# A long convolution in blocks of 256 steps instead of 128, inside a two-layer H3 and MLP kernel

## The chip, the cores and the metric

The kernel runs on one core of a Trainium2 chip. The metric is the device time of one execution, in microseconds. The core has TensorE (PE; its weight loads are shown apart, as PEld), VectorE (DVE), ScalarE (ACT), GpSimd (POOL), and SyncE (SP), which here issues all the DMAs. Each engine runs its own instructions in the order in which the program issued them.

## The reference

Two layers, each a gated long convolution and then an MLP, on 2048 tokens of 1024 channels, all in float32:

```
x = x + norm(x) * conv(x-independent kv)      # kv = shift_conv4(k) * v, causal conv with ssm_k, plus D * kv
x = x + W2 @ relu(W1 @ norm(x) + b1)**2 + b2  # 1024 -> 3584 -> 1024
```

The convolution `y` of `kv` with the 2048-step kernel `ssm_k`, per channel, takes nothing from x, so it is the same in both layers and is computed once. The reference does it with an FFT over 4096 points.

## The kernel before

The MLP. A unit is one layer on one block of 512 tokens; the eight units run in the order `ORDER = [(0,0),(1,0),(0,1),(0,2),(1,1),(1,2),(0,3),(1,3)]` (layer, block), here called u0 to u7. A unit is some 112 steps; a step uses one tile of 128x512 weights in 12 matmuls. A product of two float32 numbers is made of three fp32r matmuls (`mm3`, L271 to L273) of a high and a low part; ACT makes the high part (L685 for weights, L1030 for the activations), DVE or POOL the low part (L693, L1035). In u0 every weight is split for the first time, and part of them (`split_kept`) is stored as a pair of parts in DRAM (`wd`) and read back later. Raw weights are loaded up to 8 steps ahead into 5 buffers (`wr`).

The convolution. A block of 128 steps is taken into a spectrum with matmuls against 128-point tables of cosines and sines (odd frequencies, `fh`, `fl`); the spectrum of the filter's current block and of the one before it are combined with signs. A complex product is made of three real ones (`PAIRS`). Output block j needs the sum over i of X[i] * G[j - i]: `mult` (L407, POOL, every fourteenth on DVE) writes the products of all i, `red` (L411, DVE) sums them. `fin` then combines the three (L417, L418, POOL), splits the result into a high part yh (L426, ACT) and a low part yl (L430, DVE), transforms it back (six matmuls of 256 columns into a PSUM bank of the ring `pt`), copies it (L447, ACT) and stores it to `yd`. This is done for 16 groups of 64 channels in each of the sequence blocks 1 to 3.

The forward transforms of blocks 1 to 3 are two streams of steps, `fwd_x` (L294 to L328) and `fwd_g` (L349 to L373), in chunks of 128 channels, 24 chunks in all.

The order. Streams are generators; the main loop, at each MLP step, lets them issue as much as `pace` and `FWD_RATE` say, and `Later.at(k, ...)` issues a stage k ticks later, where a tick is one product issued. So the convolution's matmuls stand between the MLP's in TensorE's order, and its DVE and POOL instructions among the others. Blocks 1 and 2 are computed during u0 to u2, block 3 during u3 to u5; `PACE_SLACK` is the number of steps that should be left over. Eighteen steps before the end of a unit that is followed by another block, `close_conv` issues at once whatever is left of the convolution that the next unit needs.

The first block of both convolution and layer 0 (`first_block`) comes ahead of all units. There `Plan` orders the instructions from given costs and chooses DVE or POOL for those that either can do (products L907, sums L909, combinations L913 and L914).

Of the kernel before, what the change touches and what calls it, by code (L numbers as in the profile page):

```python
# [32 lines left out]
Q = 256  # L33
QC = Q // P
QG = Q // CG
PAIRS = ((2, 0), (0, 1), (1, 2))
W_LOAD, W_HI, W_LO, W_PAIR = 8, 4, 3, 5
PAIR_GAP = 10
# [9 lines left out]
PACE_SLACK = 55  # L48
# [8 lines left out]
FWD_RATE = {0: 1.3, 1: 1.2, 2: 1.2, 3: 1, 4: 0.98, 5: 1}  # L57
# [114 lines left out]
def v_cost(n):  # L172
    return 70 + 1.04 * n


def s_cost(n):
    return 130 + 1.04 * n


def g_cost(n):  # L180
    return 160 + 2.1 * n


def a_cost(n):
    return 100 + 0.84 * n
# [3 lines left out]
def tile_h3_mlp(ctx: ExitStack, tc: tile.TileContext, q, kT, vT, shk, ssmT, ssmD, w1, b1, w2, b2,  # L189
# [11 lines left out]

    XD = [dram.tile([NG, P, NBLK, CG], F32, name=f"xd{i}") for i in range(3)]
    GD = [dram.tile([NG, P, NBLK, CG], F32, name=f"gd{i}") for i in range(3)]
    KD = [[dram.tile([P, 2, Q], F32, name=f"kd{sb}_{h}") for h in range(4)] for sb in range(NB - 1)]
# [7 lines left out]
    def mkfx(shape, dt=F32):  # L212
        return cv.tile(shape, dt, name="fx", bufs=6)
# [11 lines left out]
    def const_split(name, src, shape):  # L225
        raw = mkfx(shape)
# [10 lines left out]
    fh, fl = const_split("f", fwd_t, [P, 2, P])  # L237
    ih, il = const_split("i", inv_t, [P, 2, P])
    epst = const.tile([P, 1], F32)
    V.memset(epst, EPS)  # L240

# [33 lines left out]
    def gview(t, h):  # L275
        return t.rearrange("g p b c -> p g b c")[:, QG * h:QG * h + QG]

    def hold(n):
        got = take(n)
        while not got:  # L280
            yield
            got = take(n)
        return got

    def fwd_x(sb, c):
# [17 lines left out]
        ov = o.rearrange("p (g b c) -> p b g c", g=2, b=NT)  # L303
        for b in range(NT):
            PE.transpose(ov[:, b], ks[:, b * P:(b + 1) * P], ident)
# [9 lines left out]
        xo = [mkfx([P, T]) for _ in range(3)]  # L315
        oa = yield from hold(2)
        for r in range(2):
            mm3(oa[r], fh[:, r], fl[:, r], hi, lo, True, True)
        yield
        for r in range(2):  # L320
            A.copy(xo[r], oa[r])
        yield
        V.tensor_add(xo[2], oa[1], xo[0])
        yield
        give(*oa)
        yield
        for i in range(3):
            SY.dma_start(dview(XD[i], sb, c), xo[i].rearrange("p (g b c) -> p g b c", g=2, c=CG))  # L328
        yield

    def dview(t, sb, c):
        return t[2 * c:2 * c + 2, :, NT * sb:NT * sb + NT].rearrange("g p b c -> p g b c")

    def kview(sb, c, r):
        return KD[sb][c // 2][:, r, c % 2 * P:c % 2 * P + P].rearrange("p (g c) -> p g c", c=CG)

    def fwd_g(sb, c):
        raw = mkfg([P, NT, P])
        SY.dma_start(raw, ssmT[sb * T:(sb + 1) * T, c * P:(c + 1) * P].rearrange("(b p) c -> p b c", p=P))
        kk = [mkfk([P, 2, (NT + 1) * CG]) for _ in range(2)]  # L340
        for r in range(2):
            SY.dma_start(kk[r][:, :, 0:CG], kview(sb - 1, c, r))
# [4 lines left out]
        hv, lv = (t.rearrange("p (g b c) -> p b g c", g=2, b=NT) for t in (hi, lo))  # L347
        rv = raw.rearrange("p b (g c) -> p b g c", g=2)
        A.copy(hv, rv)  # L349
        yield  # L350
        V.tensor_sub(lv, rv, hv.bitcast(F32))
# [4 lines left out]
        for r in range(2):  # L356
            mm3(oa[r], fh[:, r], fl[:, r], hi, lo, True, True)
        yield
        og = [o.rearrange("p (g n) -> p g n", g=2) for o in oa]
# [7 lines left out]
        for r in range(2):  # L367
# [968 lines left out]
```

## Time and profile before

| what | value |
|---|---|
| median of 3 runs | 3007.43 us (3004.38 to 3011.22) |
| the profiled execution, its time | 3011.77 us |
| its span, first to last instruction | 3010.0 us |
| mean granted TensorE clock | 0.96 |
| PE, DVE, POOL, ACT busy | 92%, 68%, 44%, 32% of the span |
| HBM read and written | 576.88 MB and 123.73 MB |

A row of the view by stretches gives the stretch, then the busy time of PE, PEld, DVE, ACT and POOL with the number of instructions, then the granted clock as a share of full speed, the busy share of the DMA engines and their GB/s. A row of a group gives line, engine, operation, tiles and shapes, the count, the busy time with the mean in ns, and the idle time of the engine just ahead of these instructions with what ended it. A row of a wait gives who waited for whom, the sum in us, how often, and the longest.

### The profile page before, as it was taken

The numbers are of one execution on the slowest core, as the hardware profiler recorded it, in microseconds if no ns is written. First come the engines' busy times: TensorE is split into PE (matmuls) and PEld (weight loads), VectorE is DVE, ScalarE is ACT, GpSimd is POOL, SyncE is SP. The second block draws the span as 40 slices with busy tenths as digits, with TensorE's granted clock in tenths as the row PEclk, the third lists the DMA queues.
The fourth block names the chain that finished last, engine by engine and source line by source line (L and its number), as shares of the span: only waits on it lengthen the run. The fifth ranks groups of instructions, "written<-read, shape, count | busy, mean of one in ns | idle before, by whom it ended". The sixth has DMA issues, their size and how long they took to land.

```text
span 3010.0 us, 34885 instructions
## 1 busy us (share of the span) xinstructions
PE 2774.8 (92%) x12408; PEld 2268.3 (75%) x12408; DVE 2036.8 (68%) x2624; ACT 972.5 (32%) x1658; POOL 1332.6 (44%) x768
## 2 busy tenths in 40 slices
PE   4668788869999999979999999999999999989999
PEld 3556576758778877858878888888788888878887
DVE  7967789857998799987998779886323322252221
ACT  3433333413334333323322433232223322213221
POOL 4635567635775477765667287737000100030000
PEclk7878899989999999989999999999999999999999
DMA  5457788888788987778876887687445744475444
GB/s 174 156 191 257 232 265 272 269 297 294 251 261 278 337 286 255 258 243 330 273 241 228 278 296 248 219 283 280 159 147 186 277 145 147 143 263 185 139 145 154
DMA packets 339014, 702.96 MB, mean 234 GB/s; under 512 B 75412, under 2 KB 145304, under 8 KB 338840
## 3 DMA queue, kind: packets, MB, share of 16 engines
q1 hardware_dynamic: 338840, 700.73, 69.1%
q8 instruction: 98, 1.61, 0.2%
q14 instruction: 76, 0.62, 0.1%
HBM read 576.88 MB, written 123.73 MB: 233 GB/s over the span
## 4 chain that ended last, share of the span: by engine, by line
PE 53%; DVE 6%; POOL 2%; DMA 2%; issue 1%; ACT 0%; SPq 0%; DVEq 0%; POOLq 0%; ACTq 0%
PE p L271 17%; PE p L273 17%; PE p L272 17%; POOL cp L407 1%; DVE sm L411 1%; DVE whl L693 1%; DMA yt<-yd 1%; DMA whl<-wd_m 1%; DVE fx L297 0%; PE pt L272 0%; PE pt L273 0%; DVE acc L1040 0%; PE pt L271 0%; DVE rl L1035 0%; PE p L582 0%
## 5 line engine op out<-in xcount | busy, mean ns | idle before, releaser
L407 POOL TENSOR_TENSOR cp<-cx,cg 128x320 f32<-128x320 f32 (+11 forms) x535 | 1026.4, 1944 | 637.4 <-DVE sm L411 530.3
L271 PE MATMUL p<-whl,rh 128*128 128x512 f32 x1792 | 718.5, 401 | 23.2 <-DMA whl<-wd_m 12.7
L272 PE MATMUL p<-whl,rh 128*128 128x512 f32 x1792 | 714.4, 399 | 4.3 <-DVE whl L693 4.3
L271 PE MATMUL p<-xh,whl 128*128 128x512 f32 (+1 forms) x1864 | 714.2, 383 | 1.9 <-DMA whl<-wd_m 1.4
L273 PE MATMUL p<-whl,rl 128*128 128x512 f32 x1792 | 713.6, 398 | 0.0
L272 PE MATMUL p<-xl,whl 128*128 128x512 f32 (+1 forms) x1864 | 711.3, 382 | 0.5 <-DVE xl L953 0.3
L273 PE MATMUL p<-xh,whl 128*128 128x512 f32 (+1 forms) x1864 | 710.9, 381 | 0.7 <-POOL whl L693 0.6
L1035 DVE TENSOR_TENSOR rl<-r,rh 128x512 fp32r<-128x512 f32 x224 | 251.6, 1123 | 442.2 <-ACT rh L1030 442.0
L411 DVE TENSOR_REDUCE sm<-cp 128x64 f32<-128x320 f32 (+5 forms) x576 | 473.3, 840 | 54.5 <-POOL cp L407 54.5
L693 DVE TENSOR_TENSOR whl<-wr,whl 128x512 fp32r<-128x512 f32 x397 | 418.9, 1058 | 129.5 <-ACT whl L685 122.8
L685 ACT CAST whl<-wr 128x512 fp32r<-128x512 f32 x400 | 246.7, 619 | 557.3 <-PE p L273 386.0
L271 PEld LDWEIGHTS p<-whl,rh 128*128 128x128 f32 x1792 | 341.9, 191 | 107.3 <-DMA whl<-wd_m 16.8
L271 PEld LDWEIGHTS p<-xh,whl 128*128 128x128 f32 x1864 | 354.9, 190 | 69.3 <-DMA whl<-wd_m 2.1
L273 PEld LDWEIGHTS p<-xh,whl 128*128 128x128 f32 x1864 | 354.2, 190 | 69.2 <-POOL whl L693 1.1
L272 PEld LDWEIGHTS p<-whl,rh 128*128 128x128 f32 x1792 | 342.0, 191 | 84.2 <-DVE whl L693 7.1
L272 PEld LDWEIGHTS p<-xl,whl 128*128 128x128 f32 x1864 | 354.7, 190 | 66.4 <-DVE xl L953 1.0
L273 PEld LDWEIGHTS p<-whl,rl 128*128 128x128 f32 x1792 | 341.5, 191 | 80.0
L1027 ACT ACTIVATE r<-p,b1t 128x512 f32<-128x512 f32 x221 | 152.1, 688 | 685.7 <-PE p L273 683.2
L1040 DVE TENSOR_TENSOR acc<-p,acc 128x512 f32<-128x512 f32 x240 | 160.0, 687 | 188.2 <-PE p L273 187.5
L1149 POOL TENSOR_TENSOR acc<-acc,b2t 128x1024 f32<-128x1024 f32 x24 | 62.5, 2635 | 274.5 <-DMA acc<-x 274.5
L1066 POOL TENSOR_TENSOR px<-xn,px 128x512 f32<-128x512 f32 x8 | 15.2, 1901 | 317.1 <-DVE xn L1065 317.1
L1028 ACT ACTIVATE r<-r 128x512 f32<-128x512 f32 x224 | 141.7, 633 | 7.1
(180 smaller groups left out, 2288.5 us busy)
## 6 DMA issues: line engine op xcount, KB each, us to landing
whl<-wd_m SPq DMA_DIRECT2D x528, 512.0 KB, 4.1
wr<-w SPq DMA_DIRECT2D x408, 256.0 KB, 4.3
wd_m<-whl SPq DMA_DIRECT2D x70, 512.0 KB, 4.9
cx<-xd SPq DMA_DIRECT2D x48, 512.0 KB, 4.5
cg<-gd SPq DMA_DIRECT2D x48, 512.0 KB, 6.3
xd<-fx SPq DMA_DIRECT2D x72, 256.0 KB, 5.1
cx<-xd SPq DMA_DIRECT2D x48, 384.0 KB, 4.5
cg<-gd SPq DMA_DIRECT2D x48, 384.0 KB, 5.6
```

The costliest lines, as they stand in the source:

```text
L271: PE.matmul(o, lh, rh, start=start, stop=False)
L272: PE.matmul(o, lh, rl, start=False, stop=False)
L273: PE.matmul(o, ll, rh, start=False, stop=stop)
L407: e.tensor_mul(pr.rearrange("p c i -> p i c"), xt[:, 0:j + 1], gt[:, j::-1])
L411: V.tensor_reduce(sm[:, ty, jj], st["pr"], axis=AX.X, op=OP.add)
L685: A.copy(t[:, 0], raws[n])
L693: ENG[e[n % len(e)]].tensor_sub(t[:, 1], raws.pop(n), t[:, 0].bitcast(F32))
L1027: A.activation(r, st["o"], AF.Relu, bias=b1t[:, st["f"]:st["f"] + 1])
L1028: A.activation(r, r, AF.Square)
L1035: V.tensor_sub(st["lo"], st["r"], st["hi"].bitcast(F32))
L1040: V.tensor_add(accs[tt][:, d], o, accs[tt][:, d])
L1149: G.tensor_add(a, a, b2t)
```

## The change

A block of the convolution becomes 256 steps. Its even and its odd samples are transformed apart, the even ones by the same 128-point table, the odd ones by a second table with a half-step phase (`pc`, `ps`); the sum and the difference of the two (a butterfly) are the two halves (`u`) of the 256-step spectrum. Backwards, the sum and the difference of the two halves are taken first, and each is transformed by its own table to even and odd outputs. So per sequence block there are 2 blocks instead of 4, and a column group holds 128 values (`CU`) instead of 64.

Products and reductions per group and pair fall from 4 to 2, of twice the width per block. `fin` gets two instructions more on POOL (`butterfly`), and a stage of its own for them; yh and yl are made in two halves; the inverse has 12 matmuls of 128 columns. `fwd_x` and `fwd_g` have matmuls of 256 columns, extra sums and differences on DVE, and copies on ACT; some intermediate results are written back to PSUM, and `fwd_g` holds both banks of the ring for more ticks. Even and odd tokens of a block lie in different tiles (`tokens`), for the query and the output too. In the first block, the table applies the butterfly inside the matmuls, eight chunks of 128 channels take the place of four of 256, and the two-term sums become adds that DVE or POOL can do.

Beside that: the lags of `mult`, `red` and `fin` go from 5, 7, 9 ticks to 2, 3, 4; `PACE_SLACK` and `FWD_RATE` change; the weights that are kept as pairs are all those of chunk 1, and no longer all those of the first (w1) and last (w2) chunk; raw weight buffers are 4 instead of 5; while a half unit waits for a free bank, the product stream's stages are ticked too; the planner's cost functions get other constants.

```diff
-NBLK = S // P
+BL = 256
+NBL = S // BL
+BT = T // BL
 CG = 64
 NG = D // CG
+CU = 2 * CG
...
-PACE_SLACK = 55
+PACE_SLACK = {1: 74, 3: 40}
...
+RAWS = 4
...
-FWD_RATE = {0: 1.3, 1: 1.2, 2: 1.2, 3: 1, 4: 0.98, 5: 1}
+FWD_RATE = {0: 1.4, 1: 1.4, 2: 1.4, 3: 1.1, 4: 1.1, 5: 1}
...
-        return cv.tile(shape, dt, name="fx", bufs=6)
+        return cv.tile(shape, dt, name="fx", bufs=4)
...
+    def tokens(t, b, tt):
+        return t[b * T:(b + 1) * T].rearrange("(h p s) d -> h s p d", h=BT, s=2)[tt // 2, tt % 2]
...
         oa = yield from hold(2)
+        for e in range(2):
+            for r in range(2):
+                q_ = slice(e * 256, e * 256 + 256)
+                mm3(oa[e][:, r * 256:r * 256 + 256], fh[:, 2 * e + r], fl[:, 2 * e + r], hi[:, q_], lo[:, q_], True, True)
+        yield
+        odd = mkfx([P, T])
+        A.copy(odd, oa[1])
+        yield
+        xo = cv.tile([P, 2, T], F32, name="fy", bufs=1)
+        xv = xo.rearrange("p r (n u c) -> p u (r n) c", u=2, c=CG)
+        ev = oa[0].rearrange("p (n c) -> p n c", c=CG)
+        ov = odd.rearrange("p (n c) -> p n c", c=CG)
+        V.tensor_add(xv[:, 0], ev, ov)
+        V.tensor_sub(xv[:, 1], ev, ov)
+        yield
+        give(*oa)
+        x2 = mkfx([P, T])
+        V.tensor_add(x2, xo[:, 0], xo[:, 1])
+        yield
+        yield
+        for i in range(3):
+            t = x2 if i == 2 else xo[:, i]
+            SY.dma_start(dview(XD[i], sb, c), t.rearrange("p (g b u) -> p g b u", g=2, b=BT))
+        yield
...
+    def transposes(o, ks):
+        ov = o.rearrange("p (e g b c) -> p e b g c", e=2, g=2, b=BT)
+        kv = ks.rearrange("p (b t e) -> p e b t", b=BT, e=2)
+        for e in range(2):
+            for b in range(BT):
+                PE.transpose(ov[:, e, b], kv[:, e, b], ident)
...
     def fwd_g(sb, c):
...
+            ob = oa[r].rearrange("p (b e c) -> p e b c", b=BT, e=2)
+            for e in range(2):
+                q_ = slice(e * 256, e * 256 + 256)
+                mm3(ob[:, e], fh[:, 2 * e + r], fl[:, 2 * e + r], hi[:, q_], lo[:, q_], True, True)
+        yield
         for r in range(2):
-            A.copy(kk[r][:, :, CG:], og[r])
+            A.copy(kk[r][:, BL:], oa[r])
         yield
         if sb < NB - 1:
             for r in range(2):
-                SY.dma_start(kview(sb, c, r), kk[r][:, :, NT * CG:])
-        go = [kk[1 - r][:, :, 0:NT * CG] for r in range(2)]
-        for r in range(2):
-            V.scalar_tensor_tensor(go[r], go[r], sgn[:, 1 - r:2 - r], og[r], op0=OP.mult, op1=OP.add)
-        yield
+                SY.dma_start(KD[sb][c][:, r], kk[r][:, BT * BL:])
+        V.scalar_tensor_tensor(kk[1][:, 0:T], kk[1][:, 0:T], sgn[:, 1:2], oa[0], op0=OP.mult, op1=OP.add)
+        V.scalar_tensor_tensor(oa[1], kk[0][:, 0:T], sgn[:, 0:1], oa[1], op0=OP.mult, op1=OP.add)
+        yield
+        k0 = kk[1][:, 0:T]
+        V.tensor_add(oa[0], oa[1], k0)
+        V.tensor_sub(oa[1], oa[1], k0)
+        yield
+        odd = mkfg([P, T])
+        parts = [t.rearrange("p (b e n) -> p e b n", b=BT, e=2) for t in (k0, oa[1], oa[0])]
+        odds = [parts[0][:, 1]]
+        for i in range(2):
+            odds.append(odd[:, i * BL:i * BL + BL].rearrange("p (b n) -> p b n", b=BT))
+            A.copy(odds[-1], parts[i + 1][:, 1])
+        yield
+        go = [None] * 3
+        for i in (1, 2, 0):
+            go[i] = mkfg([P, T])
+            u = go[i].rearrange("p (g b u c) -> p u b g c", g=2, b=BT, u=2)
+            ev, ov = (t.rearrange("p b (g c) -> p b g c", g=2) for t in (parts[i][:, 0], odds[i]))
+            V.tensor_add(u[:, 0], ev, ov)
+            V.tensor_sub(u[:, 1], ev, ov)
+            yield
         give(*oa)
...
-            pr = cv.tile([P, CG, j + 1], F32, name="cp", bufs=3)
+            pr = cv.tile([P, CU, j + 1], F32, name="cp", bufs=3)
...
             if k == 0:
-                ENG[FIN[sb - 1]].tensor_add(s[:, 1], s[:, 0], s[:, 1])
-                ENG[FIN[sb - 1]].tensor_sub(s[:, 2], s[:, 0], s[:, 2])
-                lag.at(2, fin, st, sm, sb, g, 1)
+                E.tensor_add(s[:, 1], s[:, 0], s[:, 1])
+                E.tensor_sub(s[:, 2], s[:, 0], s[:, 2])
+                lag.at(1, fin, st, sm, sb, g, 1)
             elif k == 1:
                 if inv[1] < inv[0]:
                     lag.at(1, fin, st, sm, sb, g, 1)
                     return
                 inv[0] += 1
-                st["yh"] = cv.tile([P, 2, NT * CG], F32R, name="yh", bufs=1)
-                A.copy(st["yh"], y)
+                st["z"] = butterfly(E, s)
                 lag.at(1, fin, st, sm, sb, g, 2)
             elif k == 2:
-                st["yl"] = cv.tile([P, 2, NT * CG], F32R, name="yl", bufs=1)
-                V.tensor_sub(st["yl"], y, st["yh"].bitcast(F32))
+                st["yh"] = cv.tile([P, 2, 2 * BT * CG], F32R, name="yh", bufs=1)
+                for e in range(2):
+                    A.copy(flat(st["yh"], e), st["z"][e])
+                lag.at(1, fin, st, sm, sb, g, 3)
+            elif k == 3:
+                st["yl"] = cv.tile([P, 2, 2 * BT * CG], F32R, name="yl", bufs=1)
+                for e in range(2):
+                    V.tensor_sub(flat(st["yl"], e), st["z"][e], flat(st["yh"], e).bitcast(F32))
                 sums[1] += 1
-                lag.at(2, fin, st, sm, sb, g, 3)
-            elif k == 3:
+                lag.at(1, fin, st, sm, sb, g, 4)
+            elif k == 4:
                 got = take(1)
                 if not got:
-                    lag.at(1, fin, st, sm, sb, g, 3)
+                    lag.at(1, fin, st, sm, sb, g, 4)
                     return
                 st["b"], = got
-                o = st["o"] = st["b"][:, :NT * CG]
-                yh, yl = st["yh"], st["yl"]
-                mm3(o, ih[:, 1], il[:, 1], yh[:, 0], yl[:, 0], True, False)
-                mm3(o, ih[:, 0], il[:, 0], yh[:, 1], yl[:, 1], False, True)
+                inverse(st["b"], st["yh"], st["yl"])
                 inv[1] += 1
-                lag.at(1, fin, st, sm, sb, g, 4)
-            elif k == 4:
-                yo = st["yo"] = cv.tile([P, NT, CG], F32, name="yo", bufs=1)
-                A.copy(yo, st["o"].rearrange("p (j c) -> p j c", c=CG))
+                lag.at(1, fin, st, sm, sb, g, 5)
+            elif k == 5:
+                yo = st["yo"] = cv.tile([P, BL], F32, name="yo", bufs=1)
+                A.activation(yo.rearrange("p (j e c) -> p e j c", j=BT, e=2),
+                             st["b"][:, 0:BL].rearrange("p (e j c) -> p e j c", e=2, j=BT), AF.Copy, scale=1.0 / BL)
...
-                            lag.at(5, mult, st, xt, gt, j, e)
-                            lag.at(7, red, st, sm, ty, jj)
-                            if ty == 2 and jj == NT - 1:
-                                lag.at(9, fin, st, sm, sb, g, 0)
+                            lag.at(2, mult, st, xt, gt, j, e)
+                            lag.at(3, red, st, sm, ty, jj)
...
+    def flat(t, e):
+        return t[:, e].rearrange("p (n c) -> p n c", c=CG)
+
+    def butterfly(E, s):
+        y = s[:, 1:3].rearrange("p r (j u c) -> p u (r j) c", u=2, c=CG)
+        E.tensor_add(flat(s, 0), y[:, 0], y[:, 1])
+        E.tensor_sub(y[:, 0], y[:, 0], y[:, 1])
+        return flat(s, 0), y[:, 0]
+
+    def inverse(o, yh, yl):
+        tabs = ((ih[:, 1], il[:, 1], ih[:, 0], il[:, 0]), (fh[:, 3], fl[:, 3], fh[:, 2], fl[:, 2]))
+        for e, (sh, sl, ch, cl) in enumerate(tabs):
+            oe = o[:, e * P:e * P + P]
+            mm3(oe, sh, sl, yh[:, e, 0:P], yl[:, e, 0:P], True, False)
+            mm3(oe, ch, cl, yh[:, e, P:], yl[:, e, P:], False, True)
...
-        if c == (0 if k == "m1" else NCH - 1):
+        if c == 1:
...
-                    pr = new(pro, "ppr", 3, [P, QG, NT * CG])
-
-                    def view(pr=pr):
-                        if jj == NT - 1:
-                            return pr.t.rearrange("p g (c i) -> p g c i", i=NT)
-                        return pr.t.rearrange("p g (i c) -> p g c i", c=CG)[:, :, :, 0:jj + 1]
-                    pl.add(opts, lambda e, xt=xt, gt=gt, view=view: ENG[e].tensor_mul(
-                        view().rearrange("p g c i -> p g i c"), xt.t[:, :, 0:jj + 1], gt.t[:, :, jj::-1]), rd, [pr])
-                    pl.add([("V", v_cost(n))], lambda e, ty=ty, view=view: V.tensor_reduce(
-                        sm.t[:, ty], view(), axis=AX.X, op=OP.add), [pr], [(sm, ty)])
-                two = [("G", g_cost(256)), ("V", v_cost(256) + VX)]
+                    pr = new(pro, "ppr", 3, [P, 2, BT, CU])
+                    pl.add(opts, lambda e, xt=xt, gt=gt, pr=pr: ENG[e].tensor_mul(
+                        pr.t, xt.t, gt.t[:, :, ::-1]), [xt, gt], [pr])
+                    pl.add([("V", v_cost(BL)), ("G", g_cost(BL) + 300)], lambda e, ty=ty, pr=pr: ENG[e].tensor_add(
+                        sm.t[:, ty], pr.t[:, :, 0], pr.t[:, :, 1]), [pr], [(sm, ty)])
...
                             fwd_tick()
+                            plag.tick()
...
+    c, s = np.cos(th), np.sin(th)
+    ph = np.pi * np.outer(2 * n + 1, 2 * f + 1) / 512.0
+    pc, ps = np.cos(ph), np.sin(ph)
     sg = np.where(np.arange(128) % 2 == 0, 1.0, -1.0)
-    c, s = np.cos(th), np.sin(th)
-    pro = np.stack([c - s, -(c + s), sg * s, sg * (c - s), sg * (c + s)], axis=1)
+    fwd = np.stack([c, -s, pc, -ps], axis=1)
+    inv = np.stack([c.T, -s.T], axis=1)
+    pro = np.stack([-pc, ps, sg * c, sg * s, sg * pc, -sg * pc, sg * ps, -sg * ps], axis=1)
```

More of the change, by code (lines that the diff above doesn't have):

```diff
@@ L302, in fwd_x @@
         o, = yield from hold(1)
-        ov = o.rearrange("p (g b c) -> p b g c", g=2, b=NT)
-        for b in range(NT):
-            PE.transpose(ov[:, b], ks[:, b * P:(b + 1) * P], ident)
+        transposes(o, ks)
         yield
@@ L346, in fwd_g @@
         lo = mkfg([P, T], F32R)
-        hv, lv = (t.rearrange("p (g b c) -> p b g c", g=2, b=NT) for t in (hi, lo))
-        rv = raw.rearrange("p b (g c) -> p b g c", g=2)
-        A.copy(hv, rv)
+        A.copy(hi, raw)
         yield
-        V.tensor_sub(lv, rv, hv.bitcast(F32))
+        V.tensor_sub(lo, raw, hi.bitcast(F32))
         yield
@@ L714, in w_advance @@
             w_hi()
-        while ptr["load"] < n and len(raws) < 5 and ptr["load"] <= w + W_LOAD:
+        while ptr["load"] < n and len(raws) < RAWS and ptr["load"] <= w + W_LOAD:
             w_load()
@@ new lines, in prods @@
+                for h in range(2):
+                    pl.add([("A", a_cost(BL))], lambda e, h=h: A.copy(flat(yh.t, h), z[h]), [(sm, h)], [(yh, h)])
+                    pl.add([("V", v_cost(BL)), ("G", g_cost(BL))], lambda e, h=h: ENG[e].tensor_sub(
+                        flat(yl.t, h), z[h], flat(yh.t, h).bitcast(F32)), [(sm, h), (yh, h)], [(yl, h)])
+                o = bank("pt", 2, pst)
+                pl.add([("PE", 820)], lambda e: inverse(o.t, yh.t, yl.t), [(yh, 0), (yh, 1), (yl, 0), (yl, 1)], [o])
@@ L1159, in tile_h3_mlp @@
     start_step = {u: (last_step[u - 1] + 1 if u else 0) for u in range(NU)}
-    work = {sb: 3 * NG * CG * 1e-3 * sum(NT * sb + jj + 1 for jj in range(NT)) for sb in range(1, NB)}
+    work = {sb: 3 * NG * CU * 1e-3 * sum(BT * sb + jj + 1 for jj in range(BT)) for sb in range(1, NB)}
     WIN = {sb: min(u for u in range(NU) if ORDER[u][1] == sb) for sb in range(1, NB)}
```

357 lines of the change are left out of this document (181 added, 176 removed).

## The prediction

> **What bounds the kernel now.** I read the busy shares first, then the clock strip, then the span cut by units (a unit is one layer on one block of 512 tokens; its end is the last relu), and last what TensorE waited for.
>
> ```profile
> PE 2774.8 (92%) x12408; PEld 2268.3 (75%) x12408; DVE 2036.8 (68%) x2624; ACT 972.5 (32%) x1658; POOL 1332.6 (44%) x768
> PEclk7878899989999999989999999999999999999999
> ```
>
> ```profile
> 0.00:183.30 183.30, 97.84 (x379) 74.49 (x379) 158.95 (x234) 70.70 (x134) 105.84 (x86) 0.75 0.47 155
> 183.30:583.10 399.80, 335.28 (x1496) 274.08 (x1496) 325.77 (x445) 153.34 (x269) 232.04 (x182) 0.91 0.79 256
> 583.10:970.10 387.00, 357.30 (x1677) 291.78 (x1677) 315.48 (x411) 125.31 (x217) 226.46 (x139) 0.96 0.82 277
> 970.10:1346.60 376.50, 351.59 (x1563) 286.55 (x1562) 343.50 (x398) 127.52 (x219) 252.98 (x138) 0.97 0.82 276
> 1346.60:1683.30 336.70, 327.56 (x1448) 267.36 (x1447) 290.80 (x316) 114.09 (x194) 208.76 (x91) 0.99 0.79 267
> 1683.30:2001.80 318.50, 318.46 (x1424) 261.82 (x1423) 257.34 (x270) 100.60 (x169) 210.04 (x92) 1.00 0.75 260
> 2001.80:2322.70 320.90, 316.06 (x1391) 259.16 (x1390) 144.76 (x219) 97.85 (x163) 61.98 (x27) 0.99 0.59 202
> 2322.70:2634.70 312.00, 312.00 (x1377) 256.05 (x1376) 91.04 (x152) 94.47 (x154) 10.37 (x4) 1.00 0.54 183
> 2634.70:2964.70 330.00, 319.73 (x1497) 265.74 (x1496) 102.91 (x174) 86.72 (x143) 24.09 (x12) 0.98 0.53 180
> ```
>
> Columns: span, busy PE, PEld, DVE, ACT, POOL, then clock, DMA share, GB/s. Row 8 (u6) is the floor: 312 us, TensorE never idle. The convolution runs beside u0 to u5. What it costs is TensorE's idle time (span less PE busy) and its half clock. Idle: u0 64.5, u1 29.7, u2 24.9, u3 9.1 us. The time at half clock is 2 x (1 - clock) x span: in u0 72 us. If all idle time fell into it, 7 us of work ran slow (4 us lost); if none, 72 (36 lost). I take 26, and in the same way 12 for u1, 6 for u2, 3 for u3. So u0 loses 90, u1 42, u2 31, u3 12: 175 us. The first row, the first block, is 183 us in which DVE is busy 87% and nothing saturates.
>
> Waits of TensorE in u0, in u1 and in u2 (total us, times, longest):
>
> ```profile
> PE pt L272 <- DVE yl L430: 34.9, 6, 6.9
> PE pt L305 <- DVE fx L299: 9.4, 4, 6.2
> ...
> PE p L271 <- DMA whl<-wd_m: 10.5, 7, 4.3
> PE p L271 <- ACT whl L685: 5.4, 2, 4.9
> ...
> PE pt L271 <- ACT yh L426: 9.6, 1, 9.6
> PE pt L272 <- DVE yl L430: 7.8, 1, 7.8
> ```
>
> In u0 it is the convolution's own matmuls, queued in TensorE among the MLP's, that wait for a DVE which runs late (81% busy).
>
> **The change, part by part.**
>
> Products. 576 products and reductions for blocks 1 to 3 become 288 of 384 to 1024 columns in equal steps, so the mean is the midpoint of these rows:
>
> ```profile
> L407 POOL TENSOR_TENSOR cp<-cx,cg 128x384 f32<-128x384 f32 x41 | 50.5, 1231 | 13.8 <-DVE sm L411 13.8
> L407 POOL TENSOR_TENSOR cp<-cx,cg 128x1024 f32<-128x1024 f32 x41 | 111.2, 2712 | 50.7 <-DVE sm L411 32.5 <-DMA yt<-yd 13.1 <-DMA wr<-w 4.7
> L411 DVE TENSOR_REDUCE sm<-cp 128x64 f32<-128x384 f32 x48 | 25.9, 539 | 0.0
> L411 DVE TENSOR_REDUCE sm<-cp 128x64 f32<-128x1024 f32 x48 | 58.0, 1207 | 4.0 <-POOL cp L407 4.0
> L407 POOL TENSOR_TENSOR cp<-cx,cg 128x320 f32<-128x320 f32 (+11 forms) x535 | 1026.4, 1944 | 637.4 <-DVE sm L411 530.3
> L411 DVE TENSOR_REDUCE sm<-cp 128x64 f32<-128x320 f32 (+5 forms) x576 | 473.3, 840 | 54.5 <-POOL cp L407 54.5
> L417 POOL TENSOR_TENSOR sm<-sm 128x256 f32<-128x256 f32 x48 | 46.7, 974 | 0.0
> L430 DVE TENSOR_TENSOR yl<-sm,yh 128x512 fp32r<-128x512 f32 x48 | 55.4, 1154 | 0.0
> ```
>
> POOL: 268 x 1.97 = 528 instead of 1026 us, plus 96 butterfly halves at 0.97 (L417's size) = 93: net -405. DVE: 288 x 0.873 = 251 instead of 473: -222. What the butterflies add on DVE is priced by these rows, the first and last with an operand in PSUM (512 and 256 columns), the others with both in SBUF:
>
> ```profile
> L323 DVE TENSOR_TENSOR fx<-pt,fx 128x512 f32<-128x512 f32 x24 | 16.4, 682 | 13.4 <-ACT fx L321 13.4
> L372 DVE TENSOR_TENSOR fg<-fk 128x512 f32<-128x512 f32 x24 | 24.9, 1039 | 0.3
> L373 DVE TENSOR_TENSOR fk<-fk 128x512 f32<-128x512 f32 x24 | 30.2, 1257 | 0.8
> L927 DVE TENSOR_TENSOR fk<-pt,cp 128x256 f32<-128x256 f32 x12 | 5.0, 420 | 6.7 <-ACT yo L929 6.1 <-PE pt L273 0.6
> ```
>
> Forward x: two 256-column PSUM adds and one 512-column SBUF add for one PSUM add, 2 x 0.42 + 1.04 - 0.68 = 1.2. Forward g: two 512-column PSUM adds for the two SBUF ones (-0.9) and six 256-column adds more, between 0.42 and 0.7 each (3.4): +2.5. For 24 chunks 24 x 3.7 = 89. The split yl in two halves (0.7 each for 1.15): 48 x 0.25 = 12; products on DVE halve, -28. Net -149. ACT gains copies (two odd halves in g, one in x), some 24 x 1.2 = 29 us, at 32% busy: hidden, unless a copy stands ahead of a weight split.
>
> Less POOL also makes DVE faster. The weight split L693 in u0, beside a POOL busy 58%, and in u6, beside 3%:
>
> ```profile
> 183.30:583.10 399.80, 100.49 (x92) 3.83 (x3) 0.91 0.79 256
> 2322.70:2634.70 312.00, 28.59 (x42) 0.00 (x0) 1.00 0.54 183
> ```
>
> 1.09 against 0.68 us. The Trainium skill (GPSIMD Engine Reference, Specifications) says that GpSimd shares VectorE's SBUF interfaces and collides with its two-input instructions; the trace agrees, by 0.41 us each.
>
> u0 by itself: DVE is busy 326 us. Its 12 groups' reductions (144 x 0.61, the mean of 320 to 512 columns) become 84 of the same mean length, since 14 groups are issued here: -36. Eight chunks' butterflies add 8 x 3.7 = 30, yl 4, and products on DVE fall by 6: 318. POOL falls from 232 to some 178 us (84 products at 1.45 for 144 at 1.34, and 28 butterfly halves), its share from 0.58 to 0.47; so about 175 two-input instructions lose 0.41 x 0.11/0.58 each, 14 us in all. DVE then needs 304; as 81.5% of the time, as now, that is 373, and nearer 360 if the stalls in which DVE stood still too become fewer. I take 36 of the 90 us back (between 0 and 65, all but a clean start). What is late next is DVE still, then the weights.
>
> u2: the stall of 9.6 + 7.8 us is the last group of block 2, which the loop that closes the block issues all at once at step 351, 18 before the unit's end. In the changed program its last step is issued at 348, so nothing is left to close (slack 74 for 55). With the slow clock behind it, 22 of 31. u1: transposes now follow their product by 2 to 6 steps (before 1 to 2), and fewer weights of the first and last chunk come back as stored pairs, the DMA wait above; in exchange ACT and DVE or POOL split them. 13 of 42, between -5 (a split is late where a DMA was) and 25. u3 4, later units 3. Together 36 + 13 + 22 + 4 + 3 = 78.
>
> TensorE: each chunk has 24 matmuls of 256 columns for 12 of 512; each of 48 groups has 12 of 128 for 6 of 256.
>
> ```profile
> 639.83 0.39 PE L272 MATMUL p<-whl,rh 128*128 128x512 f32 x1
> 640.06 0.39 PE L273 MATMUL p<-whl,rl 128*128 128x512 f32 x1
> ...
> 2685.86 0.28 PE L273 MATMUL p<-xh,whl 128*128 128x256 f32 x1
> 2685.98 0.28 PE L271 MATMUL p<-xh,whl 128*128 128x256 f32 x1
> 2337.47 0.87 PE p L582 x8
> 318.40:323.00 4.60, 4.58 (x13) 0.50 0.53 187
> ```
>
> Start to start 0.23 (0.231 over a longer stretch) and 0.12. Forward: 24 x (24 x 0.12 - 12 x 0.231) = +2.6. A 128-column matmul lies on the line through both at 0.0645, and at most at the transposes' 0.87/8 = 0.109: +2.6 to +28; I take the line, the rows of the same operands. The Trainium skill (TensorE: Matmul & The Clock Gate, Back-to-back issue gap) speaks against me: it gives some 81 ns for a sustained 128-column matmul because of its weight load. By that page the term would be +12, and the sum 9 more; no row here shows one. The last row is the clock behind the 5 us stall at 313: half speed for 4.6 us, so each stall of this size costs 2 us on top.
>
> First block, written out by the planner, which spreads work over DVE and POOL (159 + 106 us):
>
> ```profile
> L907 POOL TENSOR_TENSOR ppr<-sx,sg 128x1024 f32<-128x1024 f32 (+2 forms) x21 | 45.3, 2163 | 3.2 <-ACT sx L801 2.8 <-DVE rs L861 0.4
> L907 DVE TENSOR_TENSOR ppr<-sx,sg 128x768 f32<-128x768 f32 (+2 forms) x15 | 25.9, 1735 | 0.5 <-ACT sx L801 0.5
> L909 DVE TENSOR_REDUCE sm<-ppr 128x256 f32<-128x512 f32 (+2 forms) x36 | 34.5, 969 | 0.0
> ```
>
> These 106 us become 24 products of 512 columns (1.65), 24 adds and 12 more products of 256 (0.85): 70. But 32 butterfly halves (27), 24 spectrum sums that were copies on ACT (16 at 0.68) and more small tiles (11) come: +18 on 265. If the end moves with that, it is +12; shorter last chunks (eight of 128 channels for four of 256) may give it back. Between -10 and +25; I take +10.
>
> DMA: the tables' and loads' sizes stay; the raw weight buffers are 4 for 5, so 103 of 419 raw loads are issued 7 steps ahead of use instead of 8 (a step is 12 matmuls, 2.8 us). Costed at nothing: the split comes 4 steps ahead of use, so a load has 8 us to land. Without that cover each late one costs TensorE 1 to 3 us.
>
> Sum against the profiled execution (span 3010.0, time 3011.8; the median of the runs is 3007.4): 3011.8 - 78 + 10 + 5 = 2949; the median stands 4.4 lower, 2944. I say 2946.
>
> **Rivals.**
> Faster by more: all 175 us of u0 to u3 go, 3011.8 - 175 + 5 + 10 = 2852, or half of the rest, about 2890. For it: DVE and POOL both fall. Against: u0 keeps DVE above 75%, and seven of its groups still put the inverse one step after yl, as seven did before.
> Transfers hold it: DMA is busy 0.79 in u0 and 0.82 in u1, and ten more pair stores and two more groups come into u0. If waits on DMA replace those on DVE, only the closing stall (21) goes: 3011.8 - 21 + 15 - 4.4 = 3001.
> Slower: the butterfly waits. POOL does four instructions (3.9 us) ahead of yh, where it did two; yl sits in DVE's queue, and behind it the weight splits, so TensorE stops. Thirty-two groups run beside u0 to u2; 2.0 us each (63/32) eat the whole gain, and 3.5 us would give 3007 + 48 = 3055. Against: the butterfly has a tick of its own, and ticks are twice as long.
> That the change doesn't do what it says can be left out: the order of the instructions has half the products.
>
> **How the numbers follow.** The forecast (2895 to 2990) has 0.58, the greater gain 0.10, the transfers 0.13 (of which 0.03 end within 0.2%), the slower case 0.19. The runs lie within 0.12% of their median, so 0.2% is what can be told from no change. Faster 0.58 + 0.10 + 0.10 = 0.78, within 0.03, slower 0.19. The range leaves out the lower half of the greater gain and most of the slower case: 2880 to 3014; the likeliest alone 2895 to 2990.
>
> **What would show it.** Right: POOL near 930 us, DVE below 1950, L693's mean in u0 under 1.0 us, u0 near 360, no stall at the end of u2. Wrong: idle of PE behind yh or yl in u0 as before, a first block over 205 us, a DMA share over 0.9 with waits on weights.

## The result, and the profile after

The changed kernel takes 3092.73 us (median of 4 runs, 3090.43 to 3108.38); the kernel before, on the same chip, 3009.32 us. The ratio is 1.0291, with a 95% interval from 1.0254 to 1.0327: slower by 2.9%, where I had forecast 2% faster.

Busy shares and clock strip of the changed kernel, and its groups of products (L445) and reductions (L449, both over all six shapes):

```profile
PE 2862.2 (93%) x13512; PEld 2389.9 (77%) x13512; DVE 1713.9 (55%) x2600; ACT 979.7 (32%) x1741; POOL 882.1 (29%) x639
...
PEclk8878888888999999999999999999999999989999
...
L445 POOL TENSOR_TENSOR cp<-cx,cg 128x384 f32<-128x384 f32 (+5 forms) x268 | 482.8, 1814 | 1128.7 <-DMA cg<-gd 1043.3
```

```profile
L449 DVE TENSOR_REDUCE sm<-cp 128x128 f32<-128x384 f32 (+5 forms) x288 | 251.8, 877 | 247.7 <-POOL cp L445 247.4
```

DVE lost 323 us of work (forecast 149, and some relief by less POOL) and POOL 450 (forecast 405); in the clock strip the slices of u0 stay at 7 and 8, where before they reach 9. And POOL now stands still 1043 us for loads of cg, and DVE 247 us for products; the row of the reductions before had 54.5 us there, and that of the products had its idle time from reductions.

The stretches of the changed kernel, in the columns of before (span; busy PE, PEld, DVE, ACT, POOL; clock, DMA share, GB/s): first block, u0, u1, u2, u3, u6.

```profile
0.00:194.20 194.20, 138.71 (x912) 132.79 (x913) 154.25 (x278) 63.27 (x129) 106.76 (x120) 0.78 0.50 162
194.20:677.30 483.10, 365.62 (x1672) 302.93 (x1671) 277.13 (x434) 154.22 (x290) 155.86 (x139) 0.86 0.68 223
677.30:1082.60 405.30, 370.10 (x1822) 310.74 (x1821) 276.47 (x409) 129.81 (x239) 165.13 (x116) 0.95 0.79 263
1082.60:1430.10 347.50, 345.76 (x1649) 288.20 (x1648) 268.77 (x378) 127.92 (x234) 149.01 (x94) 1.00 0.86 295
1430.10:1764.10 334.00, 332.58 (x1553) 275.49 (x1552) 226.07 (x317) 115.50 (x205) 110.23 (x61) 1.00 0.79 270
...
2402.30:2714.30 312.00, 312.00 (x1378) 256.12 (x1377) 94.56 (x157) 94.01 (x154) 10.82 (x4) 1.00 0.54 182
```

Against before: first block +11, u0 +83, u1 +18, u2 -29, u3 -3, and the units behind within 5 us each. So, beside the 11 us of the first block, the loss is in u0 and u1. In u0 DVE has 49 us less to do than before and the unit is 83 us longer: 57% busy where it was 81%. DMA is less busy too (0.68 for 0.79). None of them is near its limit; something waits.

Waits of the changed kernel in u0 (sum in us, times, longest), then the two that answer to the first two in u0 of the kernel before:

```profile
POOL cp L445 <- DMA cg<-gd: 278.1, 34, 35.1
DVE sm L449 <- POOL cp L445: 149.3, 48, 12.3
...
PE pt L348 <- DVE fg L408: 38.1, 6, 11.4
```

```profile
POOL cp L407 <- DMA cg<-gd: 64.0, 9, 26.4
DVE sm L411 <- POOL cp L407: 41.2, 21, 8.3
```

The chain can be read off the timeline of the changed kernel (start, us, engine, line, tiles, in brackets the idle time before it; rows between these are left out):

```profile
338.09 0.68 DVE L750 TENSOR_TENSOR whl<-wr,whl 128x512 fp32r<-128x512 f32 x1
338.80 0.34 SPq L731 DMA_DIRECT2D wr<-w  x1
339.71 0.38 SPq L510 DMA_DIRECT2D cx<-xd  x1
340.15 0.96 SPq L512 DMA_DIRECT2D cg<-gd  x1
342.87 0.68 DVE L750 TENSOR_TENSOR whl<-wr,whl 128x512 fp32r<-128x512 f32 x1
343.58 0.33 SPq L731 DMA_DIRECT2D wr<-w  x1
344.48 0.38 SPq L510 DMA_DIRECT2D cx<-xd  x1
344.91 1.04 SPq L512 DMA_DIRECT2D cg<-gd  x1
345.73 2.24 POOL L445 TENSOR_TENSOR cp<-cx,cg 128x384 f32<-128x384 f32 x2 [4.81 <-DMA cg<-gd]
346.76 0.55 DVE L449 TENSOR_REDUCE sm<-cp 128x128 f32<-128x384 f32 x1 [3.22 <-POOL cp L445]
348.00 0.69 DVE L449 TENSOR_REDUCE sm<-cp 128x128 f32<-128x512 f32 x1 [0.68 <-POOL cp L445]
348.61 3.03 DVE L301 SCALAR_TENSOR_TENSOR fx<-fx,shkt 128x512 f32<-128x512 f32 x3
350.09 0.99 POOL L445 TENSOR_TENSOR cp<-cx,cg 128x384 f32<-128x384 f32 x1 [2.12 <-DMA cg<-gd]
```

The loads of a pair (340.15) go out 4.8 us ahead of the next pair's (344.91), about one MLP step. They land 5.6 us after their issue (5.4 is the median of u0), and the product starts in that moment, 345.73, having waited 4.81. The reduction stands right behind in DVE's queue and waits too; behind it stand the forward streams' steps (348.61) and the next weight splits, and SyncE lets go of its next raw weight load (338.80, 343.58) and the pair behind it only when DVE has done a split (338.09, 342.87). So each lateness is handed round: loads, product, reduction, split, loads. TensorE meets it at the end, most of all as transposes that wait for DVE's spectrum steps (38 us at L348). Its idle time in u0 (span less busy) grows from 64.5 to 117.5 us, and by the prediction's reckoning it then runs at half clock for twice (1 - 0.86) of 483, 135 us, where it was 72; half of the 63 us more is lost. Idle time and half clock together make up the 83 us.

My theory for the experiments: the lags of `mult`, `red` and `fin`, cut from 5, 7, 9 to 2, 3, 4 ticks, make the loads too late and put the reductions too close behind their products. Rivals: the other choice of kept weights, the pace, the traffic itself, SyncE's queue, the fourth raw buffer, or the larger work steps.

### The profile page after: what moved, and what is told of

Its sections match the earlier page's. It is cut to its first block, busy times and chain, and to the rows that moved or that the text cites. A ratio compares the mean times of both kernels' runs of the same rounds, so it can differ in the third digit from the quotient of the medians.

```text
span 3090.4 us, 37259 instructions
## 1 busy us (share of the span) xinstructions
PE 2862.2 (93%) x13512; PEld 2389.9 (77%) x13512; DVE 1713.9 (55%) x2600; ACT 979.7 (32%) x1741; POOL 882.1 (29%) x639
## 4 chain that ended last, share of the span: by engine, by line
PE 66%; DMA 9%; DVE 7%; POOL 2%; SPq 2%; issue 2%; ACT 1%; POOLq 0%; DVEq 0%; ACTq 0%
PE p L271 21%; PE p L273 21%; PE p L272 21%; DMA cg<-gd 4%; POOL cp L445 1%; DVE whl L750 1%; PE pt L272 1%; PE pt L273 1%; PE pt L271 1%; DMA yt<-yd 1%; DMA xd<-fx 1%; DMA wr<-w 1%; DVE sm L449 1%; PE p L639 1%; DMA wd_m<-whl 0%
## 5 line engine op out<-in xcount | busy, mean ns | idle before, releaser
L445 POOL TENSOR_TENSOR cp<-cx,cg 128x384 f32<-128x384 f32 (+5 forms) x268 | 482.8, 1814 | 1128.7 <-DMA cg<-gd 1043.3
L1113 DVE TENSOR_TENSOR rl<-r,rh 128x512 fp32r<-128x512 f32 x224 | 194.8, 870 | 547.8 <-ACT rh L1108 547.6
L750 DVE TENSOR_TENSOR whl<-wr,whl 128x512 fp32r<-128x512 f32 x408 | 349.2, 861 | 157.0 <-ACT whl L742 148.2
L742 ACT CAST whl<-wr 128x512 fp32r<-128x512 f32 x419 | 257.1, 618 | 520.4 <-PE p L273 359.7
L449 DVE TENSOR_REDUCE sm<-cp 128x128 f32<-128x384 f32 (+5 forms) x288 | 251.8, 877 | 247.7 <-POOL cp L445 247.4
L1108 ACT CAST rh<-r 128x512 fp32r<-128x512 f32 x224 | 139.1, 621 | 7.2
```

What stands on the lines that cost most here:

```text
L445: e.tensor_mul(pr.rearrange("p c i -> p i c"), xt[:, 0:j + 1], gt[:, j::-1])
L449: V.tensor_reduce(sm[:, ty, jj], st["pr"], axis=AX.X, op=OP.add)
L742: A.copy(t[:, 0], raws[n])
L750: ENG[e[n % len(e)]].tensor_sub(t[:, 1], raws.pop(n), t[:, 0].bitcast(F32))
L1108: A.copy(st["hi"], r)
L1113: V.tensor_sub(st["lo"], st["r"], st["hi"].bitcast(F32))
```

## The experiments

Times are medians; each ratio is to the kernel before on the same chip, with its 95% interval. That kernel took 3003 to 3010 us on the chips of these runs, so where two runs are compared in us, a few us may be the chip's.

**Loads earlier.** In block 1 a pair has 512 of a buffer's 1024 columns, so two pairs can share one, in the same memory:

```diff
+                        if sb > 1 or npair % 2 == 0:
+                            m = 2 if sb == 1 else 1
+                            x2 = cv.tile([P, m, nb, CU], F32, name="cx", bufs=2)
...
+                            d = 2 if sb == 1 else 0
+                            lag.at(2 + d, mult, st, xt, gt, j, e)
+                            lag.at(3 + d, red, st, sm, ty, jj)
```

> The changed kernel, but in sequence block 1 two pairs share a buffer (same size, twice as deep), so products follow their loads by 4 ticks instead of 2, reductions by 5, the combination by 6. Lead theory (products on POOL wait for loads issued too late, DVE's in-order reductions wait for them, and TensorE for DVE): DVE's wait for products in u0 falls from 149 to under 60 us, u0 from 483 to about 410, total about 3015. Rival, the banks (the forward g step holds both PSUM banks and the transposes behind it wait): u0 stays above 460, total above 3065. Rival, the weights (other pairs kept, one raw buffer less): no change, 3092.

3017.95 us, 1.0034 (1.0019 to 1.0049): 75 of the 83 us lost are back. u0 takes 417 us. Its waits:

```profile
POOL cp L446 <- DMA cg<-gd: 179.8, 32, 34.7
DVE sm L450 <- POOL cp L446: 65.1, 24, 10.4
```

**No loads.** Each block's products read the first pair loaded:

```diff
+                        if once.get("sb") != sb:
...
+                        xt, gt = once["x"], once["g"]
```

> The changed kernel with one pair of tiles loaded for a whole sequence block; all products of that block read it, so 282 of 288 loads are left out, and the output is not the convolution. Lead theory: POOL has nothing to wait for, DVE's wait for products in u0 falls under 40 us, u0 about 390, total about 2980. Banks: the 38 us of transposes waiting stay, u0 about 450, total about 3055. Weights: u0 falls only as far as DMA was short, total about 3070.

2955.65 us, 0.9835 (0.9821 to 0.985). The changed kernel's arithmetic, with every load in time, is faster than before. u0, 370 us, with 18 us more of work on DVE and 20 more on POOL than in the changed kernel:

```profile
198.40:568.10 369.70, 333.77 (x1672) 280.08 (x1671) 295.06 (x435) 153.78 (x290) 176.32 (x145) 0.96 0.71 234
```

This could still be the traffic that was left out, so later I kept the traffic and took the wait away:

```diff
+                        else:
+                            SY.dma_start(once["sx"], XD[xi][g, :, :nb])
+                            SY.dma_start(once["sg"], GD[gi][g, :, :nb])
```

> The changed kernel, whose loads for the products are all issued as before, but 282 of the 288 land in a buffer that no instruction reads; the products of a block all read the two tiles loaded first (the output is not the convolution). The traffic stays, the wait for it goes. If the wait for late loads is what the changed kernel loses, the time is within 15 us of the run in which the same loads were left out (2956 us): 2950 to 2975, and u0 near 375 us. If the load on the DMA queues or SyncE's issuing is what it loses, the gain of that run was the traffic's, and the time stays above 3050 us. SyncE now waits for a load where it writes the unread buffer again, which can cost a little.

2981.97 us, 0.993 (0.9916 to 0.9945), u0 385.5 us: 111 of the 137 us that leaving the loads out had brought. Its waits in u0, where the one for a load is the start of the stream:

```profile
POOL cp L446 <- DMA cg<-gd: 36.2, 1, 36.2
DVE sm L450 <- POOL cp L446: 16.8, 6, 12.5
```

So most of it is the wait. The upper end of my range (2975) was missed by 7 us; 26 us are the traffic's, or SyncE's, which waits 79 us in u0 to write the unread buffers again. I cannot part these two.

**The old choice of kept weights, the old pace.**

```diff
-        if c == 1:
+        if c == (0 if k == "m1" else NCH - 1):
```

> The changed kernel with the old choice of weights kept as pairs (all of the first chunk of w1 and of the last of w2). Weights theory: u0 back by 30 us or more and u1 by 15, total about 3045. Lead and banks: within 15 us of 3092, a little less in u1.

3096.74 us, 1.0302 (1.0287 to 1.0318): no part in the loss.

```diff
-PACE_SLACK = {1: 74, 3: 40}
+PACE_SLACK = {1: 55, 3: 55}
...
-FWD_RATE = {0: 1.4, 1: 1.4, 2: 1.4, 3: 1.1, 4: 1.1, 5: 1}
+FWD_RATE = {0: 1.3, 1: 1.2, 2: 1.2, 3: 1, 4: 0.98, 5: 1}
```

> The changed kernel with the old slack (55 for both) and the old forward rates. Lead theory: ticks of block 1 are some 8% longer, so u0 gains 10 to 20 us, and the closing stall at the end of u2 may come back: total 3075 to 3095. Banks: forward steps are spread out, u0 gains 30 us, total about 3060. Weights: no change.

3096.68 us, 1.0306 (1.029 to 1.0321). u0 is 463 and u1 378 us, together 47 less than in the changed kernel, and u2 381.7, 34 more, for the closing stall is back; u5 has 12 more. The new pace moves work forward into u0 and u1 and with it some of the loss, but over the whole kernel it is no cause of it.

**Reductions later.** One tick more between product and reduction, then two:

```diff
-                            lag.at(3, red, st, sm, ty, jj)
+                            lag.at(4, red, st, sm, ty, jj)
...
-                                lag.at(4, fin, st, sm, sb, g, 0)
+                                lag.at(5, fin, st, sm, sb, g, 0)
```

> The changed kernel, but a reduction is issued two ticks behind its product instead of one (lags 2, 4, 5 for 2, 3, 4). The loads of the products keep their distance. If the short distance of the loads is the cause, POOL's wait for them in u0 stays above 200 us, DVE waits less for products than 149 us but not nothing, and the time ends between 3040 and 3090 us. If the short distance between product and reduction is the cause, u0 comes down from 483 to about 400 us, DVE's wait to under 40, and the time to between 2990 and 3025 us.

3050.66 us, 1.014 (1.0121 to 1.0159), u0 454.8 us. With 5 for the reduction and 6 for the final step:

> The changed kernel with reductions three ticks behind the product (5, and 6 for the final step) and the loads still two ticks ahead of it. One tick more brought 42 us. If the distance of reductions is enough by itself, u0 falls to about 400 us and the time to between 2985 and 3025 us; if the loads, which are still late, go on to hold DVE through POOL, the time stays between 3030 and 3055 us.

3028.67 us, 1.0066 (1.0044 to 1.0089), between the two forecasts; u0 431 us. Its waits in u0:

```profile
POOL cp L445 <- DMA cg<-gd: 201.9, 34, 34.6
DVE sm L449 <- POOL cp L445: 45.3, 17, 10.3
```

POOL's wait goes down little (278 to 202) while DVE's goes from 149 to 45. So what hurts is less that POOL waits than that DVE stands in line behind it; I had given the reductions' distance too small a share.

**Both.**

```diff
+                            lag.at(2 + d, mult, st, xt, gt, j, e)
+                            lag.at(4 + d, red, st, sm, ty, jj)
...
+                                lag.at(5 + d, fin, st, sm, sb, g, 0)
```

> The changed kernel with both distances longer: in block 1 two pairs share a buffer, so loads go four ticks ahead, and reductions go two ticks behind their product everywhere. If DVE's wait of 65 us in u0 and 45 in u1, which was left with the longer loads alone (3018 us), is what that run still lost, u0 falls from 417 to under 395 us, u1 from 398 to about 380, and the time to between 2965 and 3000 us. If that wait was beside other work, the time stays between 3005 and 3025 us.

2992.34 us, 0.9946 (0.9928 to 0.9964), u0 394.3 us: faster than before. One tick more for reductions and final steps of block 1 (`4 + d + (sb == 1)`, `5 + d + (sb == 1)`):

> The version with both distances longer (2992 us), with the reductions of block 1 one tick further still, three behind their product. If DVE's remaining wait for products in u0 (40 us) still costs, u0 falls from 394 to about 385 us and the time to between 2975 and 2988 us. If the reductions are far enough, the time stays between 2988 and 2998 us; it could rise if the last group of a block ends too late.

2966.08 us, 0.9878 (0.9861 to 0.9896): faster than the kernel before by 1.2% and than the changed kernel by about 4%, and more than I expected. Its waits in u0, its stretches u0 to u3, and the same place of its timeline:

```profile
POOL cp L446 <- DMA cg<-gd: 105.8, 22, 35.1
...
POOL cp L446 <- DVE sm L450: 37.3, 21, 3.6
...
DVE sm L450 <- POOL cp L446: 9.9, 6, 6.0
```

```profile
193.70:571.80 378.10, 336.43 (x1661) 281.11 (x1659) 294.76 (x433) 153.90 (x289) 165.14 (x138) 0.95 0.84 284
571.80:956.40 384.60, 362.73 (x1826) 306.20 (x1825) 274.91 (x410) 129.36 (x239) 163.01 (x114) 0.96 0.82 278
956.40:1304.30 347.90, 345.99 (x1661) 288.39 (x1660) 277.68 (x392) 129.73 (x237) 151.83 (x96) 1.00 0.87 295
1304.30:1639.30 335.00, 333.25 (x1549) 275.61 (x1548) 219.09 (x301) 114.02 (x201) 114.13 (x62) 1.00 0.78 268
```

```profile
335.28 0.68 DVE L756 TENSOR_TENSOR whl<-wr,whl 128x512 fp32r<-128x512 f32 x1
335.88 1.13 DVE L450 TENSOR_REDUCE sm<-cp 128x128 f32<-128x384 f32 x2
335.99 0.33 SPq L740 DMA_DIRECT2D wr<-w  x1
336.50 1.30 POOL L446 TENSOR_TENSOR cp<-cx,cg 128x512 f32<-128x512 f32 x1 [2.02 <-DVE sm L450]
336.84 0.43 SPq L516 DMA_DIRECT2D cx<-xd  x1
336.94 1.41 DVE L756 TENSOR_TENSOR whl<-wr,whl 128x512 fp32r<-128x512 f32 x1
```

Here the roles have changed: POOL waits for DVE's reductions, and DVE runs from split to reduction to split without a gap, its products already made. Over u0, POOL still waits longer for loads (105.8 us) than for DVE, but DVE hardly for POOL (9.9). The two distances nearly add up, in us of the whole kernel (the 3 of the second row holds in block 1, with 2 in the later blocks):

| loads ahead of the product (block 1) | reduction 1 tick behind | 2 | 3 |
|---|---|---|---|
| 2 ticks | 3093 | 3051 | 3029 |
| 4 ticks | 3018 | 2992 | 2966 |

Read along its diagonals, the table says that what counts is the way from the loads to the reduction: 3, 4, 5, 6 and 7 ticks of it in block 1 give 3093, 3051, 3018 or 3029, 2992 and 2966 us. In u0 of the changed kernel a reduction starts 0.03 us after its product ends (median); with the longer loads alone it is 2.2 us, in the last version 4.0, and in the kernel before 2.3.

**ScalarE issues the loads.** In the changed kernel, then in the version with both distances one step longer (2992 us):

```diff
-                        SY.dma_start(xt, XD[xi][g, :, :nb])
+                        A.dma_start(xt, XD[xi][g, :, :nb])
```

> The changed kernel, but the two loads of a pair of spectra are issued by ScalarE instead of SyncE; the distances are as in the changed kernel. If the loads come late because SyncE stands ahead of them waiting for weight splits on DVE (213 us in u0), the circle is broken: u0 falls from 483 to between 370 and 420 us and the time to between 2955 and 3025 us. If the distance of two ticks is too short for the landing alone (5.4 us), POOL's wait in u0 stays above 200 us and the time stays above 3060. A price that could hide a gain: ScalarE stands still where a buffer is not yet free, and weight splits behind it.

> The version with both distances longer (2992 us), and the loads of the pairs issued by ScalarE as well. ScalarE alone took 26 us off the changed kernel, both distances 100. If ScalarE's queue mends what is left of the late loads (127 us of POOL's wait in u0), u0 falls from 394 to under 385 us and the time to between 2965 and 2988 us. If the longer distances have covered it already, ScalarE's standing still at full buffers is the only thing added, and the time is between 2990 and 3015 us.

3066.56 us, 1.0193 (1.0174 to 1.0213), and 2991.87 us, 0.994 (0.9926 to 0.9955). Taking the loads out of SyncE's queue, where they stand behind its waits for splits, brings 26 us; with the longer distances it brings none. The circle is fed by SyncE, but longer distances open it without that.

**A slower pace with both distances** (slack 70 for 74, rate in u0 1.6 for 1.4):

> The version with both distances longer, with the pace of the groups a little less hurried (slack 70 for 74) and the forward chunks of u0 a little earlier (rate 1.6 for 1.4). If groups that stand in bursts behind the forward chunks are what u0 still loses, u0 falls from 394 to about 385 us and the time to between 2975 and 2990 us; if the groups' spacing does not matter once the loads are in time, the time stays between 2988 and 3000 us. Later than slack 70 the closing stall of u2 would come back (some 20 to 30 us).

3004.51 us, 0.9991 (0.9977 to 1.0006): 12 us more than without. u0 is 2.4 us shorter, but u1 and u2 are 2.5 and 10.6 longer. A miss: less of a hurry in the groups brings nothing, so nothing here speaks for their bursts as what u0 still loses.

**The same in the kernel before.** Its lags from 5, 7, 9 to 3, 5, 7; its raw buffers from 5 to 4; and both:

```diff
-                            lag.at(5, mult, st, xt, gt, j, e)
-                            lag.at(7, red, st, sm, ty, jj)
+                            lag.at(3, mult, st, xt, gt, j, e)
+                            lag.at(5, red, st, sm, ty, jj)
```

> The kernel before, with the products' distances in time of the changed kernel: a tick of it is about half as long, and product, reduction and final step go 3, 5 and 7 ticks behind the issue of the loads instead of 5, 7 and 9. If the distance of the loads is the cause, POOL's wait for cg loads in u0 grows from 64 us to over 150, u0 from 400 to between 430 and 480, and the time to between 3035 and 3090 us. If something else of the change is the cause (the larger tiles, the butterflies on DVE, the bursts in which the groups are issued), the time stays between 2995 and 3025 us.

> The kernel before with 4 raw weight buffers instead of 5, nothing else. If the fifth buffer is only cover that is not needed, as I had costed it, the time stays within 10 us of before (3000 to 3020). If the missing buffer is a part of the loss (SyncE's wait for splits on DVE grows from 127 us in u0, and the loads for the products stand behind it), the time is between 3025 and 3070 us.

> The kernel before with 4 raw weight buffers and with the shorter distances 3, 5 and 7. The distances alone cost 52 us. If the two are one circle, together they cost more than the sum of each alone: 3080 to 3140 us. If the buffer has no part, the time is that of the distances alone, 3050 to 3075 us.

3062.04 us, 1.0176 (1.0155 to 1.0197); 3007.63 us, 1.0001 (0.999 to 1.0012); 3064.96 us, 1.0191 (1.0172 to 1.0211). In the kernel before, the buffer has no part that these runs can tell, alone or with the lags. The lags alone make it 52 us slower, without any block of 256 steps, and its u0 has the same waits (u0 424.8 us). It is only the loads that come later here: the reduction stays two ticks behind its product.

```profile
POOL cp L407 <- DMA cg<-gd: 122.5, 22, 27.5
DVE sm L411 <- POOL cp L407: 61.9, 27, 10.6
```

Of these 52 us, 25 are in u0, which is short of the 430 to 480 us expected there; the rest is spread over u1 to u4, by 6 to 11 us each.

## Why the prediction was wrong, point by point

**The step that failed** is the one that was not there: the edit of the lags has no term in the sum, which puts it at nothing without a reason. The part on DMA costed raw weight loads one step later at nothing, and that was right (the fourth buffer measures 1.0001), but it did not ask the same of the loads of cx and cg, nor of the reductions. The remark that "ticks are twice as long" stood as an argument for safety, but in u0 both ticks of a pair now mostly fall into one MLP step. In the order in which the programs issue their instructions, the first product of a pair stands two steps behind its loads in the kernel before (34 of 43 pairs of u0), and in the same step in the changed kernel (43 of 46). The loads take 5.4 us in the median to land, and a reduction stands right behind the product in DVE's queue. What this cost: POOL's wait for loads in u0 went from 64 to 278 us, DVE's for products from 41 to 149, and u0 from 400 to 483. Lengthening both distances takes the changed kernel from 3093 to 2966 us: 127 us in all.

**u0.** The forecast turned DVE's work into time with the old share: 304 us, "as 81.5% of the time, as now", 373. The work came out (277 us measured, 295 in the version of 2966 us), the share did not: 57%. With both distances longer it is 78% and u0 378 us, 14 us above the 364 (400 less 36) that the sum stood on. The share of a busy engine is no constant of a kernel; it holds only as long as what that engine waits for still comes first.

**u1** was to gain 13 and lost 18. The distances are most of it: 405 us, 385 with both longer. The gain itself is then 2 us, not 13.

**u2** gained 29 (forecast 22). The closing stall is gone: clock 1.00, idle time of TensorE 2 us. The old pace (slack and forward rates together) brings it back, so the reason given was right. **The first block** lost 11 (forecast 10), and that was luck: the forecast rested on 18 us more work for DVE and POOL there, and they have 4 less (261 us for 265), while TensorE, which the forecast for the first block leaves out, is busy 41 us longer (138.7 for 97.8). What makes the block longer is not shown. **u3** and the units behind it: within 5 us, as forecast.

**Less POOL, faster DVE.** POOL has 882 us (forecast 930), DVE 1714 (below 1950). The weight splits in u0 of the changed kernel:

```profile
194.20:677.30 483.10, 76.21 (x93) 4.21 (x3) 0.86 0.68 223
```

0.82 us each for 1.09 before (forecast: under 1.0), with POOL busy 32% for 58%. In the faster version it is 0.91 beside POOL at 44%. The relief that the Trainium skill (GPSIMD Engine Reference, Specifications) makes one expect is there; it was of no use while DVE stood still.

**TensorE** was mis-sized. The inverse's matmuls of 128 columns, in u2 of the changed kernel at full clock:

```profile
1128.43 0.28 PE L273 MATMUL pt<-yh,il 128*128 128x128 f32 x1
1128.54 0.28 PE L271 MATMUL pt<-yh,ih 128*128 128x128 f32 x1
1128.65 0.27 PE L272 MATMUL pt<-yl,ih 128*128 128x128 f32 x1
...
1129.43 0.27 PE L273 MATMUL pt<-yh,fl 128*128 128x128 f32 x1
```

Start to start 0.11 us, 0.112 as the median of 579 such: 576 x 0.112 - 288 x 0.12 = +30 us, not the +2.6 of the line through the longer ones, and just over the upper end given (28). With the forward's 2.6 the term is 33 instead of 5. These 28 us more exceed the 20 us by which the best version misses the forecast of 2946. (The prediction's own sum gives 2944; the 2 us make no difference here.)

**The rivals.** The butterfly waits did not come: none of TensorE's waits in u0 is for yh or yl any more (for yl alone it was 34.9 us). "Transfers hold it" came nearest, but by another way: no busier DMA (0.68 for 0.79) and a landing little slower (median of cg in u0 5.4 us for 5.1, of cx 5.0 for 4.4), but loads issued too late. All signs that I listed for being right came true except u0 itself, and none of those for being wrong: I had set no watch on POOL's wait for loads and DVE's for products.

**What stays open**: how the last 26 us between loads left out and loads left unread divide, and why u1 keeps 385 us where loads left out give 378. No run has the changed kernel with just the distances of the kernel before, counted in steps, or with the fifth raw buffer; that its own loss comes from the lags rests on the longer distances, on the loads left unread and on the kernel before with shorter lags.

## What to carry to other kernels

When a change halves the number of work steps, every distance that is counted in steps has to be counted again in microseconds, against the landing time and against the engine that stands in line: here a load needs some 5.4 us, and its first product stood in the same step. An in-order engine that serves several streams (DVE: reductions, splits, spectra) should not meet an operand that is made just in time; putting the consumer two or three ticks behind its producer brought 42 and 64 us here. And in a prediction, an edit that looks like a constant gets a term like any other.

## What was not expected of the hardware

A matmul of 128 columns in fp32r takes 0.112 us from start to start at full clock, 256 columns 0.12, 512 columns 0.229 (medians of the changed kernel): 128 columns save next to nothing over 256. The Trainium skill (TensorE: Matmul & The Clock Gate, Back-to-back issue gap) has some 81 ns for 128 columns; the trace shows 38% more. And issuing the loads by ScalarE instead of SyncE cost nothing that the time shows where the distances are long (2991.87 against 2992.34 us).
